# Linear attention and a mixture of experts on one core: first unit's last terms in the last pass, a fourth gating iteration ahead of the six experts, rescaling dealt out

## The chip, the core and the metric

The kernel runs on one core of one Trainium2 chip. The metric is the device time of one execution in microseconds, median of several runs; lower is better. The engines named below are TensorE (PE, with its weight loads PEld), VectorE (DVE), ScalarE (ACT), GpSimd (POOL) and SyncE (SP), whose queue issues most transfers.

## What is computed

The first half is a linear attention with a complex decay, per batch and head; its outputs are the rows x of a mixture of experts whose gate is normalised over rows and columns eight times (N = 3072 rows, 384 columns, 8 experts, 1024 hidden):

```python
    for t in range(S):
        ar, ai = (a_re_n[:, :, t, :, None], a_im_n[:, :, t, :, None])
        new_re = ar * S_re - ai * S_im
        new_im = ar * S_im + ai * S_re
        kv = np.einsum('bhd,bhe->bhde', k[:, :, t], v[:, :, t])
        S_re, S_im = (new_re + kv, new_im)
        y[:, :, t] = np.einsum('bhd,bhde->bhe', q[:, :, t], S_re)
    ...
    P = np.exp(logits)
    for _ in range(8):
        P /= P.sum(1, keepdims=True) + 1e-09
        P /= P.sum(0, keepdims=True) + 1e-09
        P *= N / E
    out = np.zeros((N, D), dtype=np.float32)
    for e in range(E):
        h = np.maximum(x @ w1[e], 0.0)
        ye = h @ w2[e]
        out += P[:, e:e + 1] * ye
```

One round of that loop over P is called a gating iteration below.

## The kernel before

**First stage (`phase1`, about 0 to 600 us).** Twelve blocks of 256 rows. For each block VectorE runs a scan, the running complex products of the decay (`cmul`, lines L400 to L405, tiles `cm_a`, `cm_b`, `z`), ScalarE and VectorE form the keys `kh` and queries in `z`, and transfers on SP (`ks`) and POOL (`qs`) bring them to the layout in which TensorE makes scores (`sp`), masked by VectorE into `sc`, the outputs `y` and the state (`tm`, `sa`, `sb`, `st`). ScalarE and VectorE split each output block into a high and a low half (`xh`, `xl`), and TensorE multiplies it by the first two experts: products `ph` (L237), halves `hh` and `hl` (L249 to L251), products `po` (L207 to L209), result `yst` (L215) stored as `ye_d`. While the experts work on a block, the scan of the next ones runs on VectorE. In this stage TensorE's order is written out by hand; the order of VectorE, ScalarE, POOL and SP is chosen when the program is built, by a scheduler that weighs the whole list of instructions, apart from some edges given by hand. So an edit of TensorE's list may order the other engines anew.

The weights of the second expert's upper half come in twelve pieces (`thirds`): loaded, their high half taken on POOL or ScalarE, the low half made by TensorE (`wd`, L183 and L184). The first `HEAD` pieces are done before the first block, with `warm` products between them, and the pieces from number `HEAD` to 7 are cast by ScalarE instead of POOL:

```python
            mid = HEAD <= n < 2 * (LAG + 1)
            ...
        for k in range(HEAD):
            if k:
                self.warm(WARM[1])
            splits.pop(0)()
```

**Gating head (`phase2a`, about 600 to 645 us).** The last block's expert products are sent one at a time by `more(k)`, and between them stand the checks, the exponential of the gate and the first `HEAD` gating iterations. One iteration is `rows` (row sums `rs`, P scaled, column sums `cs`; L720 to L724, VectorE), one product `cp` on TensorE (L728) and the rest of `columns` (L729 to L732, VectorE). The weights of the first two steps of the next stage are split there as well (`prep_w`, L878 on ScalarE, L882 on VectorE).

**Second stage (`phase2b`, from about 646 us).** Experts 2 to 7, by a scheme of fifteen products (`P1` to `P15`) for three hidden blocks times two halves of the rows. Four units u of 768 rows, each with 16 steps m (n counts them all, 0 to 63). Here the order of TensorE, VectorE, ScalarE and SP is the order in the code. A step has fifteen products `prod` (L1074 to L1076) into four banks X, Y, Z/V and P of PSUM; ScalarE copies (`copy`, L1084) and VectorE adds (`add`, L1087) gather them into tiles named `11_n`, `12_n`, `21_n`, `31_n`, `32_n`; halves `hh`, `hl` (L1095, L1096) feed the second layer (`unit`, L1021 to L1023), which runs one step later, one or two units at each of the slots `fill(0)` to `fill(14)`. Jobs listed under a slot number in `todo` are put there: weight loads and splits, the forms of the next unit's rows (`forms_late`, tiles `xb`, `xt`, `stP`, in units 1 and 2), the remaining gating iterations and others. ScalarE's copy `12_n` comes first in every step, so its start marks the step.

The result of a unit is summed over experts 2 to 7 in `oa`. Unit 0 ends before the gate is final for its first expert, so its `oa` is scaled by `rescale` (L962) later, and is stored in `od`. The terms of experts 0 and 1, `ye_d`, are added by `early`: it loads two tiles `y` (L968), for unit 0 also `od` (L971), and a step later VectorE adds them and SP stores the result (L978). `y`, `od` and `stP` take their places from one pool, `st`, with three buffers.

Of the kernel before, what the change touches and what calls it, by code (L numbers as in the profile page):

```python
# [33 lines left out]
TH = UN // 2  # L34
NS = UN // SUB
ITERS = 8
HEAD = 3
TRI = 3
NT = (E - 2) * NF // TRI
FRONT = 3  # L40
# [32 lines left out]
class Net:  # L73
# [641 lines left out]
        self.rs = sp.tile([128, ntt], F32, name="rs")  # L715
        self.cs = sp.tile([128, E], F32, name="cs")

    def rows(self):
        nc, P, rs, cs = self.nc, self.P, self.rs, self.cs
        nc.vector.tensor_reduce(rs, P, AX.X, ALU.add)  # L720
        nc.vector.tensor_scalar(rs, rs, 1e-9, None, ALU.add)
        nc.vector.reciprocal(rs, rs)
        nc.vector.tensor_tensor(P, P, rs.unsqueeze(2).broadcast_to([128, self.ntt, E]), ALU.mult)
        nc.vector.tensor_reduce(cs, P.rearrange("p t e -> p e t"), AX.X, ALU.add)  # L724

# [168 lines left out]
    def phase2a(self, c2):  # L894
        tc, nc = self.tc, self.nc
# [8 lines left out]
        n = self.N // SUB - 1  # L904
        todo = [(n, e, f) for e in range(2) for f in range(NF)][2:]

        def more(k):
            for _ in range(k):
                self.moe.send(todo.pop(0))
# [14 lines left out]
        self.sinkhorn(xa, more)  # L924
        for k in range(HEAD):
            self.rows()
            more(4 - k)
            self.columns(self.psK.tile([128, E], F32, tag="po", name=f"cp{k}"))
            if k < 2:
                prepare(k)  # L930
            if k == 0:
                self.sums(1)
                self.raw_w(2)
# [3 lines left out]
    def phase2b(self, c2):  # L937
# [22 lines left out]
        def rescale(u, k):  # L960
            tt = tile_of(u, k)
            A.activation(oa[u, k], oa[u, k], AF.Copy, scale=self.P[:, tt, 2:3])  # L962
# [65 lines left out]
        for n, (u, t) in enumerate(steps):  # L1028
# [18 lines left out]
                    todo.setdefault(5, []).append(lambda t=m + 3: self.raw_w(t, xb if t % 2 else None))  # L1047
            if u and 1 <= m < NT - 1:
                todo.setdefault(0, []).append(lambda t=steps[n + 1][1]: self.load_set(t))
            if u == 0 and m == 6:  # L1050
                for k in (3, 4, 5, 0, 1, 2):
                    rescale(0, k)
            todo.setdefault(1, []).extend(late)
            late = []
            for uu, ms in ((0, (1, 2, 4, 5, 12, 13)), (u, (6, 7, 8, 9, 10, 11))):
                if u and m in ms and (uu or u == 1):
                    y = []
                    todo.setdefault(2, []).append(lambda uu=uu, k=ms.index(m), y=y: y.append(early(uu, k)))
                    late.append(lambda y=y: y[0]())
            if 0 < n <= ITERS - HEAD:  # L1060
                todo.setdefault(6, []).append(self.rows)
            W = self.W[t]
            h = {}
            H[u, t] = (h, W)
# [1 line left out]

            def prod(nm, b, start=False):
                if start:
                    pool, tag = (self.psC, {"Z": "po0", "P": "po1", "V": "po2"}[b]) if n == 0 and b in "ZPV" else (psA, "a" if b in "XP" else "b")
                    bank[b] = pool.tile([128, TH], F32, tag=tag, name=f"{b}_{n}")  # L1070
                ps = bank[b]
                wn, k = WSLOT[nm]
                w, x = W[wn], self.X[nm]
                nc.tensor.matmul(ps, w[:, 0, k], x[:, 0], start=start, stop=False, skip_group_check=True)  # L1074
                nc.tensor.matmul(ps, w[:, 0, k], x[:, 1], start=False, stop=False, skip_group_check=True)  # L1075
                nc.tensor.matmul(ps, w[:, 1, k], x[:, 0], start=False, stop=True, skip_group_check=True)  # L1076
                if m == NT - 1 and u + 1 < NU:
                    self.swap(u + 1, nm)
# [7 lines left out]
            def add(nm, b):  # L1086
                V.tensor_tensor(c[nm], c[nm], bank[b], ALU.add)  # L1087
# [125 lines left out]
            if 0 < n <= ITERS - HEAD:  # L1213
                self.columns(psA.tile([128, E], F32, tag="a", name=f"cp{HEAD + n - 1}"))
            prod("P14", "V")
            add("31", "V")
            l21()
            l10()
            carry.append(hh(2, 0, c["31"]))
            fill(14)  # L1220
# [183 lines left out]
```

## Time and profile before

| what | value |
|---|---|
| median of 3 runs | 1777.97 us (1775.75 to 1783.97) |
| profiled execution | 1778.05 us |
| its span, first to last instruction | 1776.2 us |
| outside the span | 1.85 us |
| PE busy / PEld / DVE / ACT / POOL | 97 / 95 / 72 / 42 / 11 % |
| mean granted TensorE clock | 0.992 |

A timeline row reads: start in us, length in us, engine, line, operation, tiles out and in, shape, count; in brackets the idle time of that engine just before, and what ended it. A row of a table by stretches reads: stretch, its length, then busy time and instruction count of PE, PEld, DVE, ACT and POOL, the granted TensorE clock, the share of the DMA engines and GB/s.

### The profile page before, as it was taken

Reading aid. Unit: us, or ns where it says so; the run is one execution under the profiler, and the core shown is the slowest. Engines: PE = TensorE matmul, PEld = TensorE weight load, DVE = VectorE, ACT = ScalarE, POOL = GpSimd, SP = SyncE. Lnnn points to the kernel's source line nnn. Section 1 sums busy time; section 2 is a strip of 40 time slices with the busy share of each in tenths; the row PEclk is TensorE's granted clock in tenths of the full one; section 3 lists DMA queues with packets and bytes.
Section 4 is the critical chain, followed back from the end, with each engine's and each line's share of the span. In section 5 each row is a group of like instructions: output and inputs, shape, how many; then the busy total and the mean of one; then the engine's idle time right before and its main releaser. Section 6 shows DMA issues by size and latency. Waiting matters only on the chain.

```text
span 1776.2 us, 31227 instructions
## 1 busy us (share of the span) xinstructions
PE 1722.9 (97%) x11774; PEld 1681.9 (95%) x11774; DVE 1270.7 (72%) x2710; ACT 738.4 (42%) x1673; POOL 190.7 (11%) x360
## 2 busy tenths in 40 slices
PE   6989999999999999999998999999999999999998
PEld 4988899999999899999998999999999999999998
DVE  8988999898897678877755567666566665556654
ACT  7544454554444455544432433333433333333331
POOL 3101111111111133243300000000000000000000
PEclk9999999999999999999999999999999999999999
DMA  7434444543448776666567666658565746556550
GB/s 218 116 99 131 105 120 120 157 117 111 120 137 258 299 298 227 242 247 258 204 226 258 244 223 241 220 199 298 208 231 208 254 162 231 182 183 227 186 201 29
DMA packets 160831, 346.03 MB, mean 195 GB/s; under 512 B 15264, under 2 KB 101536, under 8 KB 160672
## 3 DMA queue, kind: packets, MB, share of 16 engines
q1 hardware_dynamic: 155264, 334.03, 54.4%
q0 software_dynamic: 4608, 9.52, 2.2%
q8 instruction: 95, 1.56, 0.3%
q14 instruction: 64, 0.52, 0.1%
q10 hardware_dynamic: 800, 0.39, 0.1%
HBM read 232.53 MB, written 98.70 MB: 186 GB/s over the span
## 4 chain that ended last, share of the span: by engine, by line
PE 82%; DVE 11%; DMA 3%; ACT 2%; issue 2%; SPq 1%; DVEq 0%; ACTq 0%
PE po L1023 11%; PE po L1021 11%; PE po L1022 11%; PE ph L237 8%; PE X L1074 4%; PE X L1076 4%; PE X L1075 4%; PE po L207 3%; PE po L209 3%; PE po L208 3%; PE Y L1074 2%; PE Y L1076 2%; PE Y L1075 2%; PE sp L580 2%; PE y L597 2%
## 5 line engine op out<-in xcount | busy, mean ns | idle before, releaser
L1023 PE MATMUL po<-wd,hl 128*128 128x384 f32 x768 | 257.3, 335 | 1.0 <-DVE hl L1096 1.0
L1022 PE MATMUL po<-wd,hh 128*128 128x384 f32 x768 | 257.0, 335 | 0.0
L1021 PE MATMUL po<-wd,hh 128*128 128x384 f32 x768 | 256.9, 335 | 0.0
L237 PE MATMUL ph<-xh,w 128*128 128x256 f32 x1152 | 227.6, 283 | 2.1 <-ACT xh L649 1.2
L237 PEld LDWEIGHTS ph<-xh,w 128*128 128x128 f32 x1152 | 186.9, 190 | 3.1 <-ACT xh L649 1.8
L249 ACT ACTIVATE hh<-ph 128x256 fp32r<-128x256 f32 x192 | 73.2, 381 | 202.6 <-PE ph L237 201.9
L237 PE MATMUL ph<-xl,w 128*128 128x256 f32 x576 | 154.7, 283 | 1.2 <-DVE xl L650 1.2
L1023 PEld LDWEIGHTS po<-wd,hl 128*128 128x128 f32 x768 | 144.5, 188 | 2.4 <-DVE hl L1096 1.9
L1021 PEld LDWEIGHTS po<-wd,hh 128*128 128x128 f32 x768 | 144.5, 188 | 0.0
L1022 PEld LDWEIGHTS po<-wd,hh 128*128 128x128 f32 x768 | 144.5, 188 | 0.0
L207 PE MATMUL po<-w,hh 128*128 128x384 f32 x384 | 141.1, 367 | 3.0 <-ACT yst L215 2.9
L209 PE MATMUL po<-w,hl 128*128 128x384 f32 x384 | 130.9, 341 | 2.6 <-DVE hl L251 2.6
L208 PE MATMUL po<-w,hh 128*128 128x384 f32 x384 | 130.0, 338 | 0.0
L1023 PE MATMUL po<-wc,hl 128*128 128x384 f32 x384 | 128.3, 334 | 0.0
L1022 PE MATMUL po<-wc,hh 128*128 128x384 f32 x384 | 128.3, 334 | 0.0
L1021 PE MATMUL po<-wc,hh 128*128 128x384 f32 x384 | 128.3, 334 | 0.0
L542 POOL DMA_DIRECT2D qs<-z x144 | 76.9, 541 | 442.3 <-ACT hf L250 81.6
L237 PEld LDWEIGHTS ph<-xl,w 128*128 128x128 f32 x576 | 106.3, 190 | 1.7 <-DVE xl L650 1.6
L1095 ACT ACTIVATE hh<-X 128x384 fp32r<-128x384 f32 x64 | 31.5, 492 | 170.5 <-PE X L1076 170.5
L251 DVE TENSOR_TENSOR hl<-hf,hh 128x256 fp32r<-128x256 f32 x192 | 81.0, 424 | 27.0 <-ACT hf L250 25.8
L1004 DVE SCALAR_TENSOR_TENSOR oa<-po,P,oa 128x384 f32<-128x384 f32 x120 | 73.1, 614 | 17.0 <-PE po L1023 16.5
L207 PEld LDWEIGHTS po<-w,hh 128*128 128x128 f32 x384 | 73.3, 191 | 8.5 <-issue 4.0
(1822 smaller groups left out, 4390.3 us busy)
## 6 DMA issues: line engine op xcount, KB each, us to landing
wd<-wd SPq DMA_DIRECT2D x58, 768.0 KB, 5.8
wa<-wd SPq DMA_DIRECT2D x42, 768.0 KB, 4.3
wb<-wd SPq DMA_DIRECT2D x42, 768.0 KB, 5.6
wc<-wd SPq DMA_DIRECT2D x42, 768.0 KB, 4.4
xP<-xf SPq DMA_DIRECT2D x60, 384.0 KB, 4.8
raw<-in_w_dram SPq DMA_DIRECT2D x12, 1152.0 KB, 8.3
wd<-wc SPq DMA_DIRECT2D x16, 768.0 KB, 4.2
wd<-wa SPq DMA_DIRECT2D x16, 768.0 KB, 4.3
```

What stands on the lines that cost most here:

```text
L207: nc.tensor.matmul(po[k], hh[:, s], w2h, start=f == 0, stop=False)
L208: nc.tensor.matmul(po[k], hh[:, s], w2l, start=False, stop=False)
L209: nc.tensor.matmul(po[k], hl[:, s], w2h, start=False, stop=f == NF - 1)
L237: nc.tensor.matmul(ph, w[:, k, ct * 128:ct * 128 + 128], x[:, ct, :], start=q == 0, stop=q == len(terms) - 1)
L251: nc.vector.tensor_tensor(hl, hf, hh.bitcast(F32), ALU.subtract)
L542: dma = eng.dma_start(dst[q:q + D - 2:NCT, :, :w], src[:, a, ct * NCH + c, :w])
L1021: nc.tensor.matmul(po[k], hh[:, s], w2[0], start=c == 1, stop=False)
L1022: nc.tensor.matmul(po[k], hh[:, s], w2[1], start=False, stop=False)
L1023: nc.tensor.matmul(po[k], hl[:, s], w2[0], start=False, stop=c == NF)
L1074: nc.tensor.matmul(ps, w[:, 0, k], x[:, 0], start=start, stop=False, skip_group_check=True)
L1075: nc.tensor.matmul(ps, w[:, 0, k], x[:, 1], start=False, stop=False, skip_group_check=True)
L1076: nc.tensor.matmul(ps, w[:, 1, k], x[:, 0], start=False, stop=True, skip_group_check=True)
```

## The change

- `HEAD` goes from 3 to 4. The head of the second stage runs four gating iterations, with 3, 2, 2 and 2 expert products ahead of their column sums instead of 4, 3 and 2; steps n = 1 to 4 hold the other four, where n = 1 to 5 held five. As `HEAD` also stands in `phase1`, four instead of three of the weight pieces are made ahead of the first block, and the fourth is cast by POOL.
- In steps 1 to 4 `rows` is cut in two: sums and reciprocal at slot 5, scaling and column sums (`rescale_rows`) at slot 10; before, all five instructions stood at slot 6.
- The six `rescale` of unit 0 stood in one piece at the start of step 6; now they stand at slots 6 to 10 and 12 of step 5.
- The terms of experts 0 and 1 for unit 0 (`early` with uu = 0, at m = 1, 2, 4, 5, 12 and 13) move from unit 1 to unit 3, the last.
- In step 0 bank X comes from pool `psD`, no longer from `psA`.
- In every step but the first, `l21` (the low half for the third hidden block's second row half) goes ahead of the last `add` of `31`.

```diff
--- before.py
+++ after.py
@@ -34,7 +34,7 @@
 TH = UN // 2
 NS = UN // SUB
 ITERS = 8
-HEAD = 3
+HEAD = 4
 TRI = 3
 NT = (E - 2) * NF // TRI
 FRONT = 3
@@ -715,11 +715,17 @@
         self.rs = sp.tile([128, ntt], F32, name="rs")
         self.cs = sp.tile([128, E], F32, name="cs")
 
-    def rows(self):
+    def rows(self, whole=True):
         nc, P, rs, cs = self.nc, self.P, self.rs, self.cs
         nc.vector.tensor_reduce(rs, P, AX.X, ALU.add)
         nc.vector.tensor_scalar(rs, rs, 1e-9, None, ALU.add)
         nc.vector.reciprocal(rs, rs)
+        if not whole:
+            return
+        self.rescale_rows()
+
+    def rescale_rows(self):
+        nc, P, rs, cs = self.nc, self.P, self.rs, self.cs
         nc.vector.tensor_tensor(P, P, rs.unsqueeze(2).broadcast_to([128, self.ntt, E]), ALU.mult)
         nc.vector.tensor_reduce(cs, P.rearrange("p t e -> p e t"), AX.X, ALU.add)
 
@@ -924,7 +930,7 @@
         self.sinkhorn(xa, more)
         for k in range(HEAD):
             self.rows()
-            more(4 - k)
+            more(3 if k == 0 else 2)
             self.columns(self.psK.tile([128, E], F32, tag="po", name=f"cp{k}"))
             if k < 2:
                 prepare(k)
@@ -1047,18 +1053,19 @@
                     todo.setdefault(5, []).append(lambda t=m + 3: self.raw_w(t, xb if t % 2 else None))
             if u and 1 <= m < NT - 1:
                 todo.setdefault(0, []).append(lambda t=steps[n + 1][1]: self.load_set(t))
-            if u == 0 and m == 6:
-                for k in (3, 4, 5, 0, 1, 2):
-                    rescale(0, k)
+            if u == 0 and m == 5:
+                for a, k in zip((6, 7, 8, 9, 10, 12), (3, 4, 5, 0, 1, 2)):
+                    todo.setdefault(a, []).append(lambda k=k: rescale(0, k))
             todo.setdefault(1, []).extend(late)
             late = []
             for uu, ms in ((0, (1, 2, 4, 5, 12, 13)), (u, (6, 7, 8, 9, 10, 11))):
-                if u and m in ms and (uu or u == 1):
+                if u and m in ms and (uu or u == NU - 1):
                     y = []
                     todo.setdefault(2, []).append(lambda uu=uu, k=ms.index(m), y=y: y.append(early(uu, k)))
                     late.append(lambda y=y: y[0]())
             if 0 < n <= ITERS - HEAD:
-                todo.setdefault(6, []).append(self.rows)
+                todo.setdefault(5, []).append(lambda: self.rows(False))
+                todo.setdefault(10, []).append(self.rescale_rows)
             W = self.W[t]
             h = {}
             H[u, t] = (h, W)
@@ -1066,7 +1073,9 @@
 
             def prod(nm, b, start=False):
                 if start:
-                    pool, tag = (self.psC, {"Z": "po0", "P": "po1", "V": "po2"}[b]) if n == 0 and b in "ZPV" else (psA, "a" if b in "XP" else "b")
+                    pool, tag = psA, "a" if b in "XP" else "b"
+                    if n == 0 and b != "Y":
+                        pool, tag = (psD, "po") if b == "X" else (self.psC, {"Z": "po0", "P": "po1", "V": "po2"}[b])
                     bank[b] = pool.tile([128, TH], F32, tag=tag, name=f"{b}_{n}")
                 ps = bank[b]
                 wn, k = WSLOT[nm]
@@ -1213,8 +1222,8 @@
             if 0 < n <= ITERS - HEAD:
                 self.columns(psA.tile([128, E], F32, tag="a", name=f"cp{HEAD + n - 1}"))
             prod("P14", "V")
+            l21()
             add("31", "V")
-            l21()
             l10()
             carry.append(hh(2, 0, c["31"]))
             fill(14)
```

SP's queue at the start of unit 1 in the kernel before, from the weights of step 17 to those of step 18. `od` and `y` are the terms of unit 0, `xb` and `xt` the forms of unit 2, `wa` to `wd` weights.

```order
L968 DMA y_12079<-ye_d_0_95 128x384
L968 DMA y_12079<-ye_d_0_119 128x384
L971 DMA od_12082<-od_163 128x384
L1006 DMA od_165<-oa_9462 128x384
L742 DMA xb_11869<-x_d_93 128x3x128
L742 DMA xt_4_12115<-x_d_93 128x3x128
L742 DMA xb_11869<-x_d_93 128x3x128
L742 DMA xt_5_12135<-x_d_93 128x3x128
L864 DMA wa_68_12230<-wd_155 128x1536
L864 DMA wb_69_12232<-wd_155 128x1536
L864 DMA wc_70_12234<-wd_155 128x1536
L864 DMA wd_71_12236<-wd_155 128x1536
```

In the changed kernel the rows of L968, L971 and L978 are gone from unit 1; in unit 3, where no forms are made, SP's queue now reads so:

```order
L974 DMA y_17495<-ye_d_0_95 128x384
L974 DMA y_17495<-ye_d_0_119 128x384
L977 DMA od_17498<-od_163 128x384
L1012 DMA out_dram<-oa_15140 128x384
L870 DMA wa_180_17636<-wd_155 128x1536
L870 DMA wb_181_17638<-wd_155 128x1536
L870 DMA wc_182_17640<-wd_155 128x1536
L870 DMA wd_183_17642<-wd_155 128x1536
L984 DMA out_dram<-od_17498 128x384
L974 DMA y_17665<-ye_d_2_97 128x384
L974 DMA y_17665<-ye_d_2_121 128x384
L977 DMA od_17668<-od_164 128x384
```

Each term's loads stand there between weights alone, and its store behind the next weights; no `xb` or `xt` is near. (Line numbers of the changed kernel are 6 to 9 higher: its L968 is the earlier L962, L974 L968, L977 L971, L984 L978, L888 L882, L1093 L1084, L1104 L1095, L735 L729.)

VectorE in the gating head, kernel before, from the row sums of the first iteration to the first column step; `wa`, `wb` are the weight splits of step 1, `hl` those of the experts' products.

```order
L722 RECIPROCAL rs<-rs 128x24
L723 TENSOR_TENSOR P<-P,rs 128x192
L882 TENSOR_TENSOR wa_5_8793<-sum_8692,wa_5_8793 128x768
L724 TENSOR_REDUCE cs<-P 128x8
L251 TENSOR_TENSOR hl_11_0_8611<-hf_11_0_8612,hh_11_0_8610 128x256
L882 TENSOR_TENSOR wb_6_8797<-raw_8370,wb_6_8797 128x128
L882 TENSOR_TENSOR wb_6_8797<-sum_8692,wb_6_8797 128x640
L251 TENSOR_TENSOR hl_11_1_8633<-hf_11_1_8634,hh_11_1_8632 128x256
L729 TENSOR_SCALAR cs<-cp_8666 128x8
L882 TENSOR_TENSOR wd_7_8803<-raw_8370,wd_7_8803 128x768
L730 RECIPROCAL cs<-cs 128x8
```

And in the changed kernel:

```order
L722 RECIPROCAL rs<-rs 128x24
L729 TENSOR_TENSOR P<-P,rs 128x192
L888 TENSOR_TENSOR wa_5_8752<-sum_8667,wa_5_8752 128x768
L730 TENSOR_REDUCE cs<-P 128x8
L251 TENSOR_TENSOR hl_11_0_8614<-hf_11_0_8615,hh_11_0_8613 128x256
L888 TENSOR_TENSOR wb_6_8756<-raw_8373,wb_6_8756 128x128
L888 TENSOR_TENSOR wb_6_8756<-sum_8667,wb_6_8756 128x640
L735 TENSOR_SCALAR cs<-cp_8641 128x8
L251 TENSOR_TENSOR hl_11_1_8636<-hf_11_1_8637,hh_11_1_8635 128x256
L736 RECIPROCAL cs<-cs 128x8
L737 TENSOR_SCALAR cs<-cs 128x8
```

VectorE's rows are the same up to the first column sums `cs`; the `cp` that L735 reads is now asked for one expert product earlier, and the split of `wd` comes later. TensorE has two expert products between every two `cp` from there on.

ScalarE from the end of step 5 to the start of step 6, before (`oa` is `rescale`):

```order
L1095 ACTIVATE hh_5_9913<-12_5_9817 128x384
L1095 ACTIVATE hh_5_9945<-X_9813 128x384
L1095 ACTIVATE hh_5_9956<-11_5_9831 128x384
L1095 ACTIVATE hh_5_9967<-21_5_9866 128x384
L878 ACTIVATE wd_28_9973<-raw_9701 128x768
L1095 ACTIVATE hh_5_9981<-32_5_9877 128x384
L962 ACTIVATE oa_9462<-oa_9462,P 128x384 x6
L1084 ACTIVATE 12_6_10017<-X_10013 128x384
```

and now:

```order
L1093 ACTIVATE 32_5_9891<-Y_9841 128x384
L968 ACTIVATE oa_9476<-oa_9476,P 128x384
L1104 ACTIVATE hh_5_9923<-12_5_9831 128x384
L968 ACTIVATE oa_9476<-oa_9476,P 128x384 x3
L1104 ACTIVATE hh_5_9958<-X_9827 128x384
L968 ACTIVATE oa_9476<-oa_9476,P 128x384
L1104 ACTIVATE hh_5_9970<-11_5_9845 128x384
L1104 ACTIVATE hh_5_9981<-21_5_9880 128x384
L884 ACTIVATE wd_28_9987<-raw_9715 128x768
L968 ACTIVATE oa_9476<-oa_9476,P 128x384
L1104 ACTIVATE hh_5_9996<-32_5_9891 128x384
L1093 ACTIVATE 12_6_10020<-X_10016 128x384
```

The six `oa` rows stand among the halves `hh` of step 5 instead of between the last of them and the copy `12_6`.

VectorE in the first stage during block 0's experts (`z2` is the scan of block 2, `sc1` and `hl1` are work for TensorE), before:

```order
L400 TENSOR_TENSOR cm_b_1529<-z2_1496 128x12x32
L251 TENSOR_TENSOR hl1_0_6_1297<-hf1_0_6_1298,hh1_0_6_1296 128x256
L404 TENSOR_TENSOR z2_1496<-cm_a_1528,cm_b_1529 128x6x32
L405 TENSOR_TENSOR z2_1496<-cm_a_1528,cm_b_1529 128x6x32
L400 TENSOR_TENSOR cm_a_1534<-z2_1496 128x12x32
L583 COPY_PREDICATED sc1_206<-mask_71,sp1_0_1_1318 128x512
L400 TENSOR_TENSOR cm_b_1535<-z2_1496 128x12x32
L404 TENSOR_TENSOR z2_1496<-cm_a_1534,cm_b_1535 128x6x32
L405 TENSOR_TENSOR z2_1496<-cm_a_1534,cm_b_1535 128x6x32
```

and now:

```order
L404 TENSOR_TENSOR z2_1499<-cm_a_1531,cm_b_1532 128x6x32
L405 TENSOR_TENSOR z2_1499<-cm_a_1531,cm_b_1532 128x6x32
L400 TENSOR_TENSOR cm_a_1537<-z2_1499 128x12x32
L400 TENSOR_TENSOR cm_b_1538<-z2_1499 128x12x32
L251 TENSOR_TENSOR hl1_0_6_1300<-hf1_0_6_1301,hh1_0_6_1299 128x256
L404 TENSOR_TENSOR z2_1499<-cm_a_1537,cm_b_1538 128x6x32
L405 TENSOR_TENSOR z2_1499<-cm_a_1537,cm_b_1538 128x6x32
L583 COPY_PREDICATED sc1_206<-mask_71,sp1_0_1_1321 128x512
```

The scheduler has put the scan's next instructions ahead of `hl1_0_6` and of the mask `sc1`; from here on most of VectorE's, ScalarE's and SP's rows of the first stage stand a few places elsewhere.

## The prediction

> **What bounds the kernel now.** I read the page's totals first, then stretches of the second stage, then the start of each step there, and only then single rows at the places that the change touches. The page:
>
> ```profile
> span 1776.2 us, 31227 instructions
> ...
> PE 1722.9 (97%) x11774; PEld 1681.9 (95%) x11774; DVE 1270.7 (72%) x2710; ACT 738.4 (42%) x1673; POOL 190.7 (11%) x360
> ...
> L1023 PE MATMUL po<-wd,hl 128*128 128x384 f32 x768 | 257.3, 335 | 1.0 <-DVE hl L1096 1.0
> ```
>
> TensorE is busy for 97% of the span, so the kernel can gain only what TensorE idles, 53.3 us, or loses at a lowered clock. Where the idle time lies is read from stretches:
>
> ```profile
> 100.00:200.00 100.00, 92.30 (x839) 87.35 (x839) 88.26 (x220) 43.40 (x112) 12.77 (x24) 0.95 0.41 118
> 740.00:1000.00 260.00, 249.85 (x1419) 247.08 (x1419) 175.69 (x331) 110.33 (x226) 49.67 (x96) 0.99 0.64 235
> 1000.00:1250.00 250.00, 247.53 (x1424) 246.17 (x1423) 158.25 (x304) 83.66 (x170) 0.00 (x0) 1.00 0.68 239
> 1250.00:1500.00 250.00, 249.88 (x1442) 249.56 (x1442) 154.65 (x297) 86.08 (x175) 0.00 (x0) 1.00 0.61 216
> 1500.00:1760.00 260.00, 259.81 (x1497) 259.17 (x1498) 148.51 (x284) 86.09 (x173) 0.00 (x0) 1.00 0.48 173
> ```
>
> From 1250 us on nothing is left (0.12 and 0.19 us idle). From 740 to 1000 us TensorE idles 10.15 us, from 1000 to 1250 us 2.47 us: that is unit 0's end and unit 1, where the change takes work away. ScalarE's copy `12_n` marks the steps; each row here is read from a short stretch of its own:
>
> ```profile
> 765.67 0.49 ACT L1084 ACTIVATE 12_7_10212<-X 128x384 f32<-128x384 f32 x1 [1.44 <-PE X L1076]
> 782.83 0.49 ACT L1084 ACTIVATE 12_8_10396<-X 128x384 f32<-128x384 f32 x1 [1.44 <-PE X L1076]
> 939.41 0.49 ACT L1084 ACTIVATE 12_17_12042<-X 128x384 f32<-128x384 f32 x1 [1.45 <-PE X L1076]
> 982.99 0.49 ACT L1084 ACTIVATE 12_19_12395<-X 128x384 f32<-128x384 f32 x1 [1.55 <-PE X L1076]
> 1017.31 0.49 ACT L1084 ACTIVATE 12_21_12740<-X 128x384 f32<-128x384 f32 x1 [1.54 <-PE X L1076]
> 1036.30 0.49 ACT L1084 ACTIVATE 12_22_12909<-X 128x384 f32<-128x384 f32 x1 [1.55 <-PE X L1076]
> 1226.85 0.49 ACT L1084 ACTIVATE 12_33_14804<-X 128x384 f32<-128x384 f32 x1 [1.43 <-PE X L1076]
> 1501.81 0.49 ACT L1084 ACTIVATE 12_49_17503<-X 128x384 f32<-128x384 f32 x1 [1.43 <-PE X L1076]
> ```
>
> An undisturbed step, 7 to 8, takes 782.83 − 765.67 = 17.16 us. Unit 1's sixteen steps (17 to 33) take 287.44 us, unit 2's (33 to 49) 274.96 us. Both units carry their own `early` and the forms of the next unit; unit 1 alone carries the terms of unit 0. The difference, 12.48 us, is their price.
>
> **The early terms, out of unit 1: −12.5.** Most of it stands in one place. Steps 17 and 18 take 43.58 us, 9.26 more than two undisturbed ones, and step 21 takes 18.99, 1.83 more. In step 18:
>
> ```profile
> 958.17 1.09 SPq L978 DMA_DIRECT2D out_dram<-od  x1
> 968.52 0.52 ACT L758 ACTIVATE stP<-xt 128x384 fp32r<-128x384 f32 x1 [8.40 <-DMA out_dram<-od]
> 969.47 0.69 PE L1074 MATMUL X<-xP,wa 128*128 128x384 f32 x1 [7.28 <-ACT 21_18_12279 L1084]
> 968.00:970.00 2.00, 0.53 (x2) 0.53 (x3) 0.93 (x2) 1.28 (x3) 0.00 (x0) 0.50 0.16 60
> ```
>
> ScalarE waits 8.40 us to write `stP`, because its buffer in `st` is still held by an `od` whose store SP issued at 958.17. The copy `21_18` is queued behind `stP`, and TensorE waits 7.28 us for that copy. Its clock is then 0.50 for a while, which makes up the other 2 us of the 9.26. With `y` and `od` out of unit 1, `stP` finds a buffer and SP is not held. What remains, 12.48 − 9.26 − 1.83 = 1.39, is spread over the steps in which VectorE has `early`'s additions between jobs that TensorE needs.
>
> **The same terms, into unit 3: +1.4.** The additions come along, so I charge the spread part again. The stall I do not charge: unit 3 makes no forms, so no `stP` asks for a buffer. An `early` of unit 0 takes `y` and `od`, the next `y` the third buffer, and its `od` waits for the first one's addition, a step after its load. SP is then held with the next step's weights behind it; those are issued a step (17 us) ahead of use, which covers it. DMA share in unit 3 is 0.48, below unit 1's 0.64 to 0.68.
>
> **Rescaling and the fifth iteration: −2.7 and −0.5.**
>
> ```profile
> 710.12 0.49 ACT L1084 ACTIVATE 12_4_9623<-X 128x384 f32<-128x384 f32 x1 [1.67 <-PE X L1076]
> 727.82 0.49 ACT L1084 ACTIVATE 12_5_9817<-X 128x384 f32<-128x384 f32 x1 [1.67 <-PE X L1076]
> 744.84 3.15 ACT L962 ACTIVATE oa<-oa,P 128x384 f32<-128x384 f32 x6 [0.98 <-DVE P L732]
> 747.89 0.47 ACT L1084 ACTIVATE 12_6_10017<-X 128x384 f32<-128x384 f32 x1
> ```
>
> Step 4, with a gating iteration, takes 17.70 us: an iteration costs 0.54. Steps 5 and 6 (727.82 to 765.67) take 37.85, 3.53 more than two undisturbed ones; less 0.54 for the fifth iteration, 2.99 is the rescaling, 3.15 us long in one piece ahead of the copy `12_6` that TensorE needs. Dealt out, each `oa` (0.53) delays one `hh` or copy by about half a microsecond. ScalarE idles elsewhere in these steps, so I leave 0.3 of it: −2.7. With four iterations in the head one is gone from the steps: −0.5.
>
> **`rows` in two: +0.4.** What an iteration in a step costs, 0.54, I share as an estimate equally between `rows`, whose five instructions hold up the additions behind slot 6, and `columns`; so 0.27 can go. New is that two of them now stand at slot 10, ahead of an addition that frees a bank:
>
> ```profile
> 628.02 0.66 DVE L723 TENSOR_TENSOR P<-P,rs 128x192 f32<-128x192 f32 x1
> 629.47 0.51 DVE L724 TENSOR_REDUCE cs<-P 128x8 f32<-128x192 f32 x1
> 669.68 0.55 DVE L1087 TENSOR_TENSOR 11_1_9036<-11_1_9036,Z 128x384 f32<-128x384 f32 x1
> 671.04 0.33 PE L1074 MATMUL V<-xP,wb 128*128 128x384 f32 x1
> ```
>
> The product V needs the bank that the addition of Z ends using at 670.23; it starts at 671.04, 0.81 later. The pair takes 0.66 + 0.51 = 1.17, so V comes 0.36 late where 0.27 was saved: about +0.1 for each of four steps. Ends: all 0.54 gone each time (−2.2), all of 1.17 lost (+4.7).
>
> **The gating head: +2.7.** The column sums `cs` are asked for after three expert products instead of four.
>
> ```profile
> 630.71 0.28 PE L728 MATMUL cp<-cs,ones 128*128 128x8 f32 x2
> 635.00 0.52 DVE L724 TENSOR_REDUCE cs<-P 128x8 f32<-128x192 f32 x1
> 637.26 0.28 PE L728 MATMUL cp<-cs,ones 128*128 128x8 f32 x2
> 642.01 0.39 PE L728 MATMUL cp<-cs,ones 128*128 128x8 f32 x2
> ```
>
> Between the first two `cp` lie three products, 6.55 us, so a product takes about 2.14. One fewer puts TensorE at `cp` at 628.57, but the first `cs` ends at 629.98, and the order of VectorE up to it is unchanged: a wait of 1.4. The second `cs` ends at 635.52, 5.54 after the first, with the same instructions between in the changed order; TensorE has two products and `cp`, 4.4: a wait of 1.1. The third had two products ahead of its `cp` before as well (637.26 to 642.01, 4.75, where two products and `cp` take 4.4), so for the third and fourth I add 0.2 together. Sum +2.7; ends 0 (VectorE's rows move up as TensorE asks sooner) and 5.4 (the third and fourth wait like the first two, since the split of `wd` now lies later). The products themselves are only moved.
>
> **Bank X in step 0 and `l21`: −0.1 and −0.2.**
>
> ```profile
> 655.98 0.45 PE L1074 MATMUL X<-xP,wc 128*128 128x384 f32 x1 [1.67 <-DVE hl L1096]
> 659.05 0.55 DVE L1087 TENSOR_TENSOR 11_1_9036<-11_1_9036,X 128x384 f32<-128x384 f32 x1
> 660.26 0.33 PE L1074 MATMUL X<-xP,wb 128*128 128x384 f32 x1
> ```
>
> The first X of step 1 waits 1.67 for a half `hl` that reads step 0's X. With step 0's X in another pool it need not. But a later X of step 1 (660.26) needs an addition that ends at 659.60 in a chain of VectorE work that does not move: 0.66 slack, so some 0.6 of the 1.67 is real, and the new bank is shared with the last eviction of the first stage, about one ScalarE copy of 0.49. Net −0.1, ends −1.7 and +0.5. `l21` one place earlier removes part of the 1.0 that L1023 waited for `hl` over all steps: −0.2, ends 0 and −1.0; the addition pushed behind it is a 0.55 row and has the slack of the V bank.
>
> **The first stage: −2.0.** `HEAD` stands there too, and the scheduler has moved the scan ahead of `hl` and `sc` from block 0's experts on. The extra split and its `warm` ahead of block 0 are work moved from later, and I cost them at nothing: TensorE waits there for the first keys anyway. What the new order can reach are stalls like these:
>
> ```profile
> 123.25 0.65 PE L209 MATMUL po<-w,hl 128*128 128x384 f32 x1 [1.84 <-DVE hl L251]
> 120.00:125.00 5.00, 3.16 (x17) 2.84 (x17) 4.94 (x13) 1.17 (x5) 0.00 (x0) 0.83 0.19 74
> 192.67 2.05 PE L580 MATMUL sp<-qs,ks 112*128 112x128 f32 x8 [2.41 <-DMA qs<-z]
> ```
>
> The second follows a late scan (`z` to `qs`), and a scan that is ahead by some VectorE instructions should shorten it; the first is a wait for `hl`, which now comes after more of the scan and may grow. In sum the stretch 100 to 200 us has 7.7 us to gain. I take −2.0, nearest to the 2.41 row; ends −8 (all 7.7) and +6 (the wait of 1.84 three times more, in as many blocks).
>
> What a short wait takes beside its own length is shown by the same rows: 1.84 us of idle, and a granted clock of 0.83 over 5 us, 0.85 us lost. If the head's two waits cost that each, the sum is 1.7 higher; I leave it to rival 4, since the clock dip may belong to the busy VectorE stretch as a whole with its several waits. [...]
>
> **Sum.** −12.5 + 1.4 − 2.7 − 0.5 + 0.4 + 2.7 − 0.1 − 0.2 − 2.0 = −13.5. The profiled execution took 1778.05 us, its span and 1.85 around it, 0.1 above the median of the runs; so 1764.5.
>
> **Rivals.** Half a per cent, 8.9 us, is about what a measurement of this kernel tells from no change: faster is below 1769.1, slower above 1786.9.
> 1. The forecast, 1760 to 1769: 0.58.
> 2. The first stage loses its stall at 192.67 and the lowered clock around it as well: −8 there instead of −2, 1758.5. For it speaks that the scan moves ahead, against it that `hl` moves back: 0.15.
> 3. The stall moves with its cause. In unit 3 `od` waits for buffers, SP is held, and weights come late: 9.26 + 1.83 again, 1775.6. Against it: no `stP`, and a step of cover. 0.06.
> 4. The first stage gets worse, or the head's waits also take clock: +6 instead of −2, or 1.7 on top, 1766 to 1772.5. 0.18.
> 5. Slower: `hl`, `sc` and the mask stand behind scan instructions in every block. From −13.5 to +8.9 are 22.4 us, so it decides at one more wait of 2.04 us in each of eleven blocks; at 2.1 us it gives 1764.5 + 23.1 = 1787.6. VectorE is 88% busy from 100 to 200 us, so a delay is made up slowly; against it, the row of 1.84 is the longest such wait. 0.03.
>
> About half of rival 4's 0.18 lies above 1769.1, with rival 3 and the forecast's own upper edge that makes 0.22 for the same and 0.75 for faster. The range, 1756 to 1773, holds the cases 1, 2 and 4 and leaves out 3 and 5 and the tails of 2 and 4.
>
> **What would show it.** Steps 17 to 19 about 34.4 us with no `out_dram<-od` ending a wait of ScalarE; unit 3 about 1.4 longer than before, TensorE above 99% busy; steps 5 and 6 near 34.6; two waits of TensorE for `cs` of 1 to 1.5 us in the head. The prediction is wrong if TensorE idles over 2 us at one place in unit 3, or if the first stage ends over 6 us from where it ended.

## The result and the profile after

The changed kernel takes 1760.7 us (median of 5 runs, 1759.71 to 1764.63), the kernel before 1778.87 (5 runs). The ratio is 0.990, 95% interval 0.988 to 0.9921: 18 us faster. The time lies 3.8 us below the 1764.5 that was forecast, and inside the range. The forecast counted from 1778.05, so 17.35 us are to be explained against its 13.5. The profiled execution took 1760.35.

The page of the changed kernel, the same lines as before:

```profile
span 1758.5 us, 31221 instructions
...
PE 1716.2 (98%) x11778; PEld 1675.0 (95%) x11778; DVE 1273.6 (72%) x2710; ACT 738.7 (42%) x1672; POOL 190.3 (11%) x361
...
L1029 PE MATMUL po<-wd,hl 128*128 128x384 f32 x768 | 257.2, 335 | 0.8 <-DVE hl L1105 0.8
```

The stretches of the second stage after (the last one ends 20 us sooner than the one shown of before):

```profile
740.00:1000.00 260.00, 258.71 (x1485) 256.88 (x1484) 178.75 (x335) 111.07 (x227) 49.68 (x96) 1.00 0.65 238
1000.00:1250.00 250.00, 249.88 (x1441) 249.33 (x1440) 155.52 (x299) 85.75 (x174) 0.00 (x0) 1.00 0.65 230
1250.00:1500.00 250.00, 249.88 (x1442) 249.56 (x1441) 155.85 (x299) 84.80 (x172) 0.00 (x0) 1.00 0.61 216
1500.00:1740.00 240.00, 239.20 (x1378) 238.56 (x1377) 141.69 (x270) 79.22 (x159) 0.00 (x0) 1.00 0.54 192
```

TensorE's idle time from 740 to 1000 us went from 10.15 to 1.29 us, that from 1000 to 1250 from 2.47 to 0.12. What came back in unit 3 is below a microsecond of idle. Now the places, by rows of short stretches. First what ends the first stage (`mp`, the maximum of the gate's logits), then step 0, before and after:

```profile
619.50 0.27 PE L705 MATMUL mp<-ident,mx 128*1 128x128 f32 x1
646.23 0.49 ACT L1084 ACTIVATE 12_0_8914<-X 128x384 f32<-128x384 f32 x1 [0.60 <-PE X L1076]
656.82 0.49 ACT L1084 ACTIVATE 12_1_9021<-X 128x384 f32<-128x384 f32 x1 [0.75 <-PE X L1076]
1742.20 0.49 ACT L1084 ACTIVATE 12_63_19790<-X 128x384 f32<-128x384 f32 x1 [1.55 <-PE X L1076]
```

```profile
613.60 0.27 PE L705 MATMUL mp<-ident,mx 128*1 128x128 f32 x1
624.10 0.39 PE L734 MATMUL cp<-cs,ones 128*128 128x8 f32 x2 [1.24 <-DVE cs L730]
629.51 0.39 PE L734 MATMUL cp<-cs,ones 128*128 128x8 f32 x2 [0.67 <-DVE cs L730]
642.93 0.44 PE L1083 MATMUL X<-xP,wc 128*128 128x384 f32 x1 [0.58 <-ACT yst L215]
643.80 0.49 ACT L1093 ACTIVATE 12_0_8928<-X 128x384 f32<-128x384 f32 x1 [0.93 <-PE X L1085]
653.53 0.48 ACT L1093 ACTIVATE 12_1_9035<-X 128x384 f32<-128x384 f32 x1
657.22 0.44 PE L1083 MATMUL X<-xP,wb 128*128 128x384 f32 x1 [0.64 <-DVE 11_1_9050 L1096]
724.50 0.49 ACT L1093 ACTIVATE 12_5_9831<-X 128x384 f32<-128x384 f32 x1 [1.62 <-PE X L1085]
741.79 0.49 ACT L1093 ACTIVATE 12_6_10020<-X 128x384 f32<-128x384 f32 x1 [0.93 <-PE X L1085]
760.36 0.49 ACT L1093 ACTIVATE 12_7_10215<-X 128x384 f32<-128x384 f32 x1 [1.44 <-PE X L1085]
933.50 0.49 ACT L1093 ACTIVATE 12_17_12045<-X 128x384 f32<-128x384 f32 x1 [1.43 <-PE X L1085]
967.82 0.49 ACT L1093 ACTIVATE 12_19_12385<-X 128x384 f32<-128x384 f32 x1 [1.55 <-PE X L1085]
1208.62 0.49 ACT L1093 ACTIVATE 12_33_14759<-X 128x384 f32<-128x384 f32 x1 [1.45 <-PE X L1085]
1483.58 0.49 ACT L1093 ACTIVATE 12_49_17458<-X 128x384 f32<-128x384 f32 x1 [1.43 <-PE X L1085]
1569.38 0.49 ACT L1093 ACTIVATE 12_54_18292<-X 128x384 f32<-128x384 f32 x1 [1.55 <-PE X L1085]
1587.24 0.49 ACT L1093 ACTIVATE 12_55_18466<-X 128x384 f32<-128x384 f32 x1 [1.55 <-PE X L1085]
1725.22 0.49 ACT L1093 ACTIVATE 12_63_19793<-X 128x384 f32<-128x384 f32 x1 [1.54 <-PE X L1085]
```

The differences of neighbouring rows give the account of the two traces:

| stretch | before | after | difference |
|---|---|---|---|
| first stage, to `mp` | 619.50 | 613.60 | −5.90 |
| head, `mp` to `12_0` | 26.73 | 30.20 | +3.47 |
| step 0 | 10.59 | 9.73 | −0.86 |
| steps 1 to 4 | 71.00 | 70.97 | −0.03 |
| steps 5 and 6 | 37.85 | 35.86 | −1.99 |
| steps 7 to 16 | 173.74 | 173.14 | −0.60 |
| unit 1 from step 17 to 33 | 287.44 | 275.12 | −12.32 |
| unit 2 from step 33 to 49 | 274.96 | 274.96 | 0 |
| step 49 to 63 | 240.39 | 241.64 | +1.25 |
| from step 63 to the end of the span | 34.00 | 33.28 | −0.72 |

Steps 17 and 18 take 34.32 us, two undisturbed ones. The extra in unit 3 stands in two steps: step 54 takes 17.86 instead of 17.24, step 62 likewise. From step 63 to the end of the span it is 33.0 to 34.0 us in the fourteen traces of this document; 0.25 of the last row of the table belongs to `l21` (below), the rest is scatter. Two things were left to tell apart: the first stage gained more than the forecast gave it, and the head, unit 0 and the rest of the change nearly cancel.

### The profile page after: what moved, and what is told of

Same layout as the page of the kernel before. It is cut to its first block, busy times and chain, and to the rows that moved or that the text cites. A ratio compares the mean times of both kernels' runs of the same rounds, so it can differ in the third digit from the quotient of the medians.

```text
span 1758.5 us, 31221 instructions
## 1 busy us (share of the span) xinstructions
PE 1716.2 (98%) x11778; PEld 1675.0 (95%) x11778; DVE 1273.6 (72%) x2710; ACT 738.7 (42%) x1672; POOL 190.3 (11%) x361
## 4 chain that ended last, share of the span: by engine, by line
PE 85%; DVE 9%; DMA 2%; ACT 2%; issue 1%; SPq 0%; POOL 0%; DVEq 0%; ACTq 0%
PE po L1029 11%; PE po L1028 11%; PE po L1027 11%; PE ph L237 9%; PE X L1083 4%; PE X L1084 4%; PE X L1085 4%; PE po L207 3%; PE po L209 3%; PE po L208 3%; PE Y L1083 2%; PE Y L1084 2%; PE Y L1085 2%; PE sp L580 2%; PE y L597 2%; PE V L1083 1%
## 5 line engine op out<-in xcount | busy, mean ns | idle before, releaser
L1104 ACT ACTIVATE hh<-X 128x384 fp32r<-128x384 f32 x64 | 31.5, 492 | 176.0 <-PE X L1085 176.0
L1105 DVE SCALAR_TENSOR_TENSOR hl<-X,hh 128x384 fp32r<-128x384 f32 x64 | 35.7, 558 | 62.3 <-ACT hh L1104 62.3
```

## The experiments

All experiments run beside the kernel before. Where only a profile was taken, steps are compared and not times; an undisturbed step repeats to 0.03 us between traces. The head does not: with the order of before it takes 26.73 to 27.34 in four traces, with that of the changed kernel 29.86 to 30.35 in six; among the four the third wait for `cs` is anything from 0 to 0.75. The diffs show changed lines alone and leave out what stands between them.

**One part alone: the constant in the first stage.** The new order of the first stage follows from this constant alone: with it at 4 or 3 in `phase1` and `thirds`, the order of every engine up to the gating head is that of the changed kernel or of the kernel before.

```diff
+HEADP = 4
-            mid = HEAD <= n < 2 * (LAG + 1)
+            mid = HEADP <= n < 2 * (LAG + 1)
-        for k in range(HEAD):
+        for k in range(HEADP):
```

> The kernel before with one edit: four instead of three weight pieces ahead of the first block (the constant as it stands in the first stage alone), everything from the gating head on as before. Theory A, the new order of the first stage makes the gain seen up to the gating head (5.9 us): the wait of 2.4 us for the queries near 190 us and the lowered clock behind it are gone, the gating's first maximum stands at about 613.6 instead of 619.5, steps of the second stage as before, about 1773. Rival B, that wait is a matter of the run and not of the order: no wait in some runs of either, 1777 to 1779. Rival C, most of the gain came from the head and the steps after it: under 2 us here.

Measured 1774.74 (10 runs) against 1778.82 (13 runs): ratio 0.9974, interval 0.9962 to 0.9985, 4.1 us. `mp` at 615.90. The gain goes the way of theory A, but is less than its 5.9. Behind `mp` this trace takes 1.7 us more than that of before up to step 63: 0.6 in the head, 1.1 in the stall of steps 17 and 18, which is there again (44.67).

**The part taken out of the change:** `HEADP = 3` with all else as changed.

> The changed kernel with three weight pieces ahead of the first block again; the rest as changed. Theory A: the wait for the queries near 190 us is back, with a granted clock under 0.8 behind it; 1760.7 + 5.9 = 1766.6. Rival B: no such wait, 1760 to 1762.

1765.01 (4 runs), 4.3 above the changed kernel's 1760.7, but its profiled execution took 1761.56, with `mp` at 615.09 in the very order that gave 619.50 before. So neither A nor B alone: the order counts, and something that varies from run to run counts as much. The stretches 190 to 195 and 195 to 200 us show it. First the kernel before with only the terms moved (`early_only`, below), then this one, with the row of its wait, which ended ahead of the stretches; both have the first stage of before:

```profile
190.00:195.00 5.00, 3.07 (x13) 3.10 (x14) 4.86 (x12) 0.26 (x2) 1.63 (x4) 0.70 1.06 235
195.00:200.00 5.00, 5.00 (x43) 4.87 (x44) 4.76 (x18) 2.61 (x8) 0.00 (x0) 0.96 0.63 199
```

```profile
189.27 1.12 PE L581 MATMUL sp<-qs,ks 112*128 112x128 f32 x6 [1.69 <-issue]
190.00:195.00 5.00, 5.00 (x32) 5.00 (x31) 4.83 (x14) 1.64 (x4) 0.00 (x0) 0.68 1.03 276
195.00:200.00 5.00, 5.00 (x49) 4.67 (x47) 4.72 (x24) 1.47 (x6) 0.00 (x0) 1.00 0.56 159
```

The kernel before had 0.66 in both stretches in the trace shown in the prediction: the same order and a wait of TensorE at the same product, and the low clock lasts up to twice as long. With the order of the changed kernel that wait is gone, but another stands at 223: `po` waits 2.03 us for `hl`. Here the changed kernel and `p1_only`, the row of the wait and the three stretches behind it:

```profile
223.91 0.44 PE L209 MATMUL po<-w,hl 128*128 128x384 f32 x1 [2.03 <-DVE hl L251]
220.00:225.00 5.00, 2.97 (x22) 2.61 (x21) 4.94 (x10) 2.35 (x7) 0.00 (x0) 1.00 0.48 156
225.00:230.00 5.00, 5.00 (x37) 4.85 (x36) 5.00 (x8) 1.40 (x5) 3.82 (x8) 1.00 0.66 153
230.00:235.00 5.00, 5.00 (x38) 5.00 (x38) 4.59 (x13) 1.32 (x4) 2.43 (x5) 1.00 1.00 251
```

```profile
222.87 0.44 PE L210 MATMUL po<-w,hl 128*128 128x384 f32 x1 [2.04 <-DVE hl L252]
220.00:225.00 5.00, 2.96 (x18) 2.64 (x18) 4.94 (x9) 1.30 (x4) 0.00 (x0) 0.91 0.34 88
225.00:230.00 5.00, 5.00 (x21) 4.75 (x20) 4.10 (x7) 0.84 (x3) 4.87 (x10) 0.50 0.93 180
230.00:235.00 5.00, 5.00 (x35) 5.00 (x34) 2.73 (x7) 1.32 (x4) 1.38 (x3) 0.91 0.74 216
```

The wait is the same to 0.01 us; in the one it costs 2.0 us, in the other the clock behind it is also 0.50 for most of 7 us (21 products in five busy microseconds instead of 37). Of nine traces with the new order seven show the dip, two do not, the changed kernel's own among those two. The profiled pair thus overstates the first stage. The wait of 1.84 us at 123.25 that the prediction shows is of this sort as well: the four other traces with the old order have it too (1.83 or 1.84), and their clock stays at 1.00 from 115 to 135 us, where the trace of before fell to 0.50. With the new order that wait is 0.86.

**One part alone: the terms of experts 0 and 1 into unit 3.**

```diff
-                if u and m in ms and (uu or u == 1):
+                if u and m in ms and (uu or u == NU - 1):
```

> The kernel before with one edit: the terms of experts 0 and 1 for unit 0 are added in unit 3 instead of unit 1. Theory: steps 17 to 19 take 34.3 instead of 43.6, unit 1 about 275.1, unit 3 1.2 longer; 1778.9 - 12.3 + 1.2 = 1767.8. Rival: a transfer wait of a few us appears in unit 3 and the gain is under 6. The order of the first stage is that of before, so its trace also shows whether the wait near 190 us is there again.

1767.19 (4 runs), ratio 0.9938 (0.9917 to 0.996), 11.6 us. Steps 17 to 19 take 34.32, unit 1 275.12, step 49 to 63 1.2 more than before. The wait for the queries is there again (2.36 us at 191.93). This is what the theory had.

**The other way to end the stall: a buffer for `od`, the terms left in unit 1.**

```diff
+        odp = c2.enter_context(tc.tile_pool(name="odp", bufs=1))
-                o = self.st.tile([128, 2, C], F32R, tag="st", name=f"od{tt}").bitcast(F32)[:, 0]
+                o = odp.tile([128, C], F32, tag="od", name=f"od{tt}")
```

> The kernel before with one edit: the tile od has a pool of its own with one buffer, instead of a place among the three of st. The terms stay in unit 1. Theory, the stall of step 18 is the wait for a buffer: stP finds one, steps 17 to 19 take 34.3, the rest of unit 1's extra (3.1) stays, 1778.9 - 9.3 = 1769.6. Rival, SP held by the stores and late transfers: the stall stays above 3 us, since SP's order is the same and od now waits for the od before it.

1767.11 (4 runs), as much as moving the terms. ScalarE's write of `stP` in step 18, 8.40 us late before, follows at once, and steps 17 and 18 take 34.31:

```profile
939.74 0.49 ACT L1085 ACTIVATE 12_17_12045<-X 128x384 f32<-128x384 f32 x1 [1.43 <-PE X L1077]
960.34 0.52 ACT L758 ACTIVATE stP<-xt 128x384 fp32r<-128x384 f32 x1
974.05 0.49 ACT L1085 ACTIVATE 12_19_12398<-X 128x384 f32<-128x384 f32 x1 [1.55 <-PE X L1077]
```

Step 21 loses its 1.83 too, so 11.1 of the 12.48 were waits for that pool of three buffers (the expectation had 9.3), and only some 1.2 is VectorE's additions, which cost the same in unit 1 as in unit 3 (steps 22 and 30 here at 17.84 and 17.85, steps 54 and 62 there). SP's queue and the transfers were not the cause.

**Three iterations in the head again,** 4, 3 and 2 products, five in the steps, and so the rescaling in one piece ahead of step 6. `HEADP = 4`, used as above, keeps the first stage of the changed kernel.

```diff
-HEAD = 4
+HEAD = 3
+HEADP = 4
-            more(3 if k == 0 else 2)
+            more(4 - k)
-            if u == 0 and m == 5:
-                for a, k in zip((6, 7, 8, 9, 10, 12), (3, 4, 5, 0, 1, 2)):
-                    todo.setdefault(a, []).append(lambda k=k: rescale(0, k))
+            if u == 0 and m == 6:
+                for k in (3, 4, 5, 0, 1, 2):
+                    rescale(0, k)
```

> The changed kernel with three gating iterations in the head again (4, 3 and 2 expert products ahead of the column sums) and five in steps 1 to 5, and the rescaling in one piece ahead of step 6, where the gate is then final; first stage, terms, rows in two, bank X and l21 as changed. Theory: the fourth iteration in the head costs TensorE 1.9 us of recorded waits and some slower products behind them, 3.5 us in all from the gate's maximum to step 0 (30.2 against 26.7 before), and saves 0.54 in step 5 and 1.5 by the earlier rescaling: head 26.7 to 27.3, steps 5 and 6 37.4 to 37.9, together about 1 us faster than the changed kernel, 1759.7. Rival: the head gains nothing from the fewer waits, since VectorE is what it is limited by, and the kernel is 2 us slower than changed, 1762.7.

1761.8 (4 runs), ratio 0.9902 (0.9886 to 0.9919). The head takes 28.42 instead of 30.20, steps 5 and 6 37.80 instead of 35.86: −1.78 and +1.94. Head and steps are even; the fourth iteration ahead brought nothing by itself. The steps came out as expected (37.4 to 37.9), the head did not (26.7 to 27.3): it gained little over half, since one `cs` was late here as well (0.93) and the wait of 0.58 for `yst`, which comes with bank X, stayed. By time the kernel lies between the theory (1759.7) and the rival (1762.7).

**The rescaling in one piece ahead of step 6,** four iterations in the head: the last six lines of the diff above alone.

> The changed kernel with the rescaling in one piece ahead of step 6. The prediction put 2.99 us on it: steps 5 and 6 then take 38.5 to 38.9 instead of 35.86. Rival: part of step 6's extra belongs to VectorE's sums of oa in that step, which ran inside the wait for the rescaling: 37.1 to 37.5, so that the rescaling was worth 1.5.

Steps 5 and 6 take 36.57, 0.71 more than dealt out. Neither the prediction's 2.99 nor the rival's 1.5: dealing it out is worth 0.7, the fifth iteration gone and the gate final a step sooner 1.2 (37.80 less 36.57), and of the 3.53 that these steps had over undisturbed ones, 1.54 are still there. By steps, the changed kernel takes 2.78 us less in step 5 and 0.79 more in step 6, which takes 18.57 instead of 17.78. In step 6 VectorE forms the first six sums `oa` (0.61 each) between additions that free banks. Before, the first of the six ran ahead of the copy `12_6` (747.89), while the rescaling held that copy up; now it runs behind the copy (741.79) like the others:

```profile
746.99 0.62 DVE L1004 SCALAR_TENSOR_TENSOR oa<-po,P,oa 128x384 f32<-128x384 f32 x1
743.17 0.61 DVE L1010 SCALAR_TENSOR_TENSOR oa<-po,P,oa 128x384 f32<-128x384 f32 x1
```

So the wait hid one sum of six; with the other five, step 6 was 0.62 over an undisturbed step before as well.

**Bank X back in `psA`.**

```diff
-                    pool, tag = psA, "a" if b in "XP" else "b"
-                    if n == 0 and b != "Y":
-                        pool, tag = (psD, "po") if b == "X" else (self.psC, {"Z": "po0", "P": "po1", "V": "po2"}[b])
+                    pool, tag = (self.psC, {"Z": "po0", "P": "po1", "V": "po2"}[b]) if n == 0 and b in "ZPV" else (psA, "a" if b in "XP" else "b")
```

> The changed kernel with bank X of step 0 back in psA. From the gate's maximum to the copy of step 0 0.6 us less (TensorE need not wait for yst), step 0 10.6 instead of 9.73 (the wait of 1.67 for hl is back): sum 0.3 us slower. Rival: the new bank is worth nothing or less, since the wait for yst cancels it.

Head 29.31 (−0.89), step 0 10.58 (+0.85), step 1 17.60 (−0.38): 0.4 us less than changed. Of the 0.89 in the head 0.58 is the wait for `yst`; the rest is within the head's scatter, so the new bank costs 0.1 to 0.4. The rows above show why: TensorE waits 0.58 for `yst` ahead of step 0 and 0.64 for the addition of `11_1`.

**`rows` in one piece at slot 6, and `l21` behind the addition,** each undone alone.

```diff
-                todo.setdefault(5, []).append(lambda: self.rows(False))
-                todo.setdefault(10, []).append(self.rescale_rows)
+                todo.setdefault(6, []).append(self.rows)
```

> The changed kernel with rows in one piece at slot 6 of steps 1 to 4. The prediction had the split cost 0.1 a step, 0.4 in all, so steps 1 to 4 (70.97 as changed) would take 70.5. Rival: the split saves what rows held up, and they take 71.3 or more.

```diff
-            l21()
             add("31", "V")
+            l21()
```

> The changed kernel with l21 behind the last addition of 31 in every step, as before. The prediction put 0.2 us on it over all steps: steps 7 to 63 together 0.2 longer. Rival: no step changes by more than 0.02, and l21 had no one waiting for it.

With `rows` whole, steps 1 to 4 take 71.98 instead of 70.97: the split saves 1.0. A row of VectorE in it, and what GpSimd did meanwhile:

```profile
686.23 0.65 DVE L729 TENSOR_TENSOR P<-P,rs 128x192 f32<-128x192 f32 x1
684.66 2.53 POOL L847 TENSOR_TENSOR sum<-raw 128x256 f32<-128x256 f32 x5
```

At slot 10 no GpSimd row overlaps the scaling of P, and it takes 0.35. With `l21` late, steps 1 to 4 take 70.56 (0.4 less), steps 5 and 6 0.36 less, steps 9 and 14 0.6 more; from step 0 to 63 it is 0.2 us shorter. Behind step 63 it is 0.25 longer: TensorE's last product ends 26.37 to 26.41 us after `12_63` in the five traces with `l21` late, 26.12 or 26.13 in the nine with it early. Its move moved time around and brought nothing.

**Two further versions.** `best1`: unit 0's terms in other steps of unit 3, and no sum of `oa` at two slots ahead of additions that free a bank.

```diff
-            for uu, ms in ((0, (1, 2, 4, 5, 12, 13)), (u, (6, 7, 8, 9, 10, 11))):
+            for uu, ms in ((0, (0, 1, 2, 3, 4, 12)), (u, (6, 7, 8, 9, 10, 11))):
-                if fin and (s < 8 or s in (9, 10, 11)):
+                if fin and (s < 8 or s in (9, 10, 11)) and (u or s not in (1, 5)):
```

> The changed kernel with two edits: unit 0's terms go to steps 0, 1, 2, 3, 4 and 12 of unit 3 instead of 1, 2, 4, 5, 12 and 13, so that their additions do not fall into steps 6 and 14 of the unit, where VectorE sums oa; and in unit 0 no sum is put at slots 1 and 5, just ahead of additions that free a bank. Theory: steps 54 and 62 take 17.24 instead of 17.86, step 6 under 18.1 instead of 18.57, step 14 under 17.7; 2 us faster than changed, 1758.7. Rival: the sums pushed back come late for the bank that the next products need, and unit 0 is no shorter: 1759.5 to 1760.7.

1758.96 (4 runs), ratio 0.9885 (0.9868 to 0.9901). Steps 54 and 62 take 17.23, step 6 17.51, step 14 17.16: from `mp` to step 63 1108.32 us, 3.3 less than changed, as the theory had it and a little more. `best2` adds bank X in `psA`, and another spacing of the head:

```diff
-            more(3 if k == 0 else 2)
+            more((4, 2, 2, 1)[k])
+            if k == HEAD - 1:
+                self.moe.send((None, None, None))
...
         more(len(todo))
-        self.moe.send((None, None, None))
```

> best1 with bank X of step 0 back in psA, and in the head 4, 2, 2 and 1 expert products ahead of the column sums, the last product of column sums behind the last second-layer products. Theory: bank X cost 0.4 over head and steps 0 and 1 as changed, and the first wait for cs (1.24) is gone while the others stay under 0.7 each; from the gate's maximum to step 0 27.6 to 28.6 instead of 30.3, step 0 10.6; 1.5 us less than best1, 1757.5. Rival: the column step of the fourth iteration now runs on VectorE at the start of step 0 and holds up its additions, 1 us or more, and nothing is gained.

Head 27.89 with waits for `cs` of 0.24 and 0.57, step 0 10.59; from `mp` to step 63 1106.34, 5.3 less than changed. By time 1758.84 (5 runs, 1755.19 to 1761.88), not to be told from `best1`, nor either surely from the changed kernel's 1759.71 to 1764.63. In the trace of `best2_p3` (below), with the same order in the head, a wait for `cs` is 1.39 and the head 28.72, so the 0.57 and the 27.89 are not sure either. The clock of the first stage hides such a step: up to `mp`, these two traces lost 7.7 and 7.6 us to it, the changed kernel's 1.7 (worked out from stretches of 1 us, busy time times one minus the granted clock, summed).

**`best2` with the first stage of before,** `HEADP = 3`, on the same chip.

> best2 with three weight pieces ahead of the first block, so the first stage has the order of before: all else equal, on the same chip. Theory D, the order is worth 1 to 2.5 us and the rest of what the two first profiles differ by (5.9 us) is the granted clock of that run: 1 to 2.5 us slower than best2, with a wait for the queries near 190 us and none of 2 us near 223. Theory A, the order itself brings 4 us or more: over 1761. Rival: no difference between the two.

1762.94 (4 runs, 1761.67 to 1764.11), 4.1 above `best2`. Third comparison of the two orders, third time about 4 by the medians (4.1, 4.3, 4.1). By time that is theory A (4 or more, over 1761); the traces speak for D. The wait for the queries is there (2.52 at 191.36), none of 2 us stands near 223, and `mp` comes 1.3 us later than in `best2`; another 1.2 us arose up to step 63, in code that is the same. Over all traces `mp` stands at 618.6 on average for the five with the old order (615.1 to 619.8), 616.5 for the nine with the new one (613.6 to 620.2); less the time lost to the clock 612.4 and 611.4. So some 1 us is waits and about as much again a clock that is low less often (6.2 us lost on average against 5.1). With `mp` spread over 4.7 and 6.6 us within one order, these means are not clear of scatter, and the last 2 us that the times show are not placed.

## Why the prediction was right, term by term

The direction and the main mechanism held: moving the terms brought 11.6 of the 17 us by time, 11.1 of unit 1's 12.3 being the waits that the prediction named, and the first stage brought about 4. The size was 3.8 short, most of it in the first stage. That the rest came out close is partly luck: from `mp` to step 63 the terms add up to −11.5 and the traces differ by −11.1, because the rescaling was taken 1.2 too large and `rows` 1.4 the wrong way. Of the signs that it named, steps 17 to 19, unit 3 and the first wait for `cs` came; steps 5 and 6 (35.86, not 34.6) and the second wait (0.67) did not.

- *Early terms out of unit 1, −12.5:* −12.32. The wait for a buffer in step 18 is shown by the kernel with a buffer of its own for `od`. The split inside the term was a little off: step 21's 1.83 went with the buffer too.
- *The same terms in unit 3, +1.4:* +1.25, in steps 54 and 62; no `stP`, no stall. Rival 3 did not happen.
- *Rescaling and the fifth iteration, −3.2:* −1.99. The term was too large: it took all that steps 5 and 6 had above two undisturbed ones, less one iteration, for the rescaling. But 0.62 of it was step 6's, beside VectorE's sums of `oa`, and the one sum that the wait had hidden now falls into step 6 as well, which keeps 1.4.
- *`rows` in two, +0.4:* −1.0, the wrong sign. The saving was sized right (0.27 a step, measured 0.25). The step that failed is the price, by a duration: the scaling of P was taken at 0.66 us from a row of the head that a GpSimd `sum` overlaps. At slot 10 none does, and it takes 0.35, the pair 0.87 instead of 1.17 against 0.81 of slack. V is not late. (The three edits in steps 1 to 4, undone one by one, give 71.2 in sum; before had 71.00, so they hardly act on each other.)

```profile
684.00 0.35 DVE L729 TENSOR_TENSOR P<-P,rs 128x192 f32<-128x192 f32 x1
684.38 0.52 DVE L730 TENSOR_REDUCE cs<-P 128x8 f32<-128x192 f32 x1
684.82 0.54 DVE L1096 TENSOR_TENSOR 11_2_9249<-11_2_9249,Z 128x384 f32<-128x384 f32 x1
685.42 0.45 PE L1083 MATMUL V<-xP,wb 128*128 128x384 f32 x1
```

- *Gating head, +2.7:* with bank X as before 29.31 against 26.73, +2.6, or +2.3 against the mean of four traces with the head of before. The two waits are 1.24 and 0.67 where 1.4 and 1.1 were worked out, so the sum came out better than its parts; what makes up the rest is not shown.
- *Bank X, −0.1, and `l21`, −0.2:* +0.1 to +0.4, and about 0 (+0.2 to step 63, −0.25 behind it). For bank X the forecast saw both waits (for `11_1`, 0.6, and for `yst`) and netted them a little too well.
- *First stage, −2.0:* 4.1 by time; −2.06 in the mean of fourteen traces, −5.9 in the two first ones. The stall at 192.67 is gone as forecast, and a wait for `hl` grew from 0.80 (at 229.47) to 2.03, though not the one shown, which fell from 1.84 to 0.86. So the term was sized at half of what the times show. The time, 1760.7, stands at the lower edge of the forecast's 1760 to 1769 and nearer to rival 2's 1758.5 than to 1764.5, but not for rival 2's reason: the clock dip left with the wait in two of nine traces and came back behind the other wait in seven. The first stage ended 5.90 us from where it had, just under the 6 at which the prediction called itself wrong; as two runs of one first stage lie up to 6.6 apart, that sign could not tell.

No cost by the head's waits in the clock was seen: no stretch of 5 us from 600 us to step 0 has a clock below 1.00 in any of the traces. The 1.7 us that the prediction worked out for them from the row of 1.84, and left to rival 4, did not come; the four other traces of that order, too, have its wait (1.83 or 1.84) with a clock of 1.00.

## What to carry to other kernels

When a unit of work costs more than its twin, subtract the twin step by step, and look in the row of the stall for what is held and by whom: here a pool shared by three tiles of different lives held up ScalarE for 8.40 us, and one buffer more did as much as moving the work (1767.11 us against 1767.19). Price a moved piece only after asking what runs inside the wait that it ends; here that was one sum of `oa`, 0.61 us, and it was late next. And where one trace of each is compared, look at the granted clock in the stretches that differ before an order of instructions is given the credit.

## What the hardware showed

A wait of one length had two prices here. Behind the same 2.03 us of idle at the same instruction the clock was 1.00 in two of nine traces and 0.50 for most of 7 us in seven; the wait of 2.2 to 2.9 us for `ks` near 92 us went with a clock of 1.00 from 90 to 95 us in some traces and of 0.66 to 0.86 in others. Two runs of one first stage differ by up to 6.6 us at `mp` (613.60 and 620.18), and 5.1 of it is time lost to the clock (1.7 and 6.8). What decides in a given run, the runs do not show.

VectorE's scaling of P (128x192) had two durations as well. In the fourteen traces it takes 0.35 or 0.36 us in all 58 rows that no GpSimd row overlaps, and 0.62 to 0.66 in 49 of the 54 that a row of GpSimd, its `sum`, overlaps. Moving it from slot 6 to slot 10, clear of the `sum`, took it from 0.65 to 0.35 in the rows shown above.
